# Interleaving the first two output groups of a feed-forward block, and who squares its last step

## The chip, the cores and the metric

The kernel runs on one core of one Trainium2 chip. The metric is the device time of one execution in microseconds; the number compared is the median over several runs. The engines are TensorE (PE in the profile; PEld is its weight load), VectorE (DVE), ScalarE (ACT), GpSimd (POOL) and SyncE (SP), which issues the stores. They run side by side and wait for each other by semaphores.

## What is computed

The input `x` has 8 sequences of 3008 rows of 256 values. The reference takes the Fourier transform along both axes, keeps the real part, and sends each of the 24064 rows through a feed-forward net with squared ReLU:

```python
X = np.fft.fft(np.fft.fft(x, axis=1), axis=2).real    # (8, 3008, 256)
rows = X.reshape(8 * 3008, 256)
h = np.maximum(rows @ w_in, 0.0)                       # (24064, 2048)
out = (h * h) @ w_out                                  # (24064, 256)
```

Matmuls run on 16-bit operands with 32-bit sums; the output is 32-bit.

## The kernel before, in words

*The symmetry.* The real part of the transform of real data needs only half of the rows: row k and its mirror row S - k come from the same two parts, a cosine part C and a sine part Z, one as their sum and one as their difference. The kernel folds each sequence (VectorE, lines 364 to 497), transforms the folded rows with matmuls against sine and cosine tables (`z_steps`, L548) into `zc` and `zs`, and folds the transform along the other axis into `w_in` (`gh`, L499). So FFN1 for the pair of rows is C plus Z for the one and C minus Z for the other.

*Blocks and steps.* The 12040 pairs of rows are cut into 25 blocks `w` (L74, called windows there): 240, 512, 376, 376, 512, 448, then eighteen of 512, and a last one of 360. In a block of n pairs, the hidden layer `h2` is a tile of 128 partitions x 16 chunks x 2n columns: the first n columns of each chunk belong to the one row of the pair (`sg` 0), the next n, in mirrored order, to the other (`sg` 1). FFN1 of a block is eight steps `s` (loop at L965), each making two of the 16 chunks. FFN2 of a block takes groups of 128 columns of `h2` as weights, 16 matmuls of 256 columns per group, one per chunk (L684); it runs one block later. A block of 512 has eight groups; groups 0 to 3 are `sg` 0. `ffn2_steps` (L668) gives a list of jobs of four matmuls, `part(i, hf)` for group i and chunks 4 hf to 4 hf + 3, and `spread` (L713) shares them evenly over the eight steps of the next block: four jobs, so sixteen matmuls, a step. Before the change the jobs stand group after group, so step 0 reads all 16 chunks of group 0, the two chunks of the last block's step 7 among them. Two groups share one PSUM bank `po`, one half each; after the second one's last job ScalarE copies it to `osb` (L699) and SyncE stores it.

*An ordinary step* (L987 on): four matmuls make C + Z in PSUM (`pq`, L831 and L832); ScalarE rectifies it into `sg` 0 (`relu`, L863); FFN2's sixteen matmuls of the step follow (`others`, L881); two turn matmuls (`turn`, L854) take away twice Z in the same PSUM tile; ScalarE rectifies again into `sg` 1. VectorE squares both halves in place in one pass (`power`, L870), which is put off to the next step by `keep` and `settle`.

*A `diff` step* (L967 on), in the steps that the table `diff` (L725) names for a block, saves the turn matmuls. Two matmuls make C (`cosines`, L840); VectorE computes the Nyquist row's share less 2 C into `t2` (`twice`, L844), from products that GpSimd has made before (`nyq_rows`, L792, into one of three buffers `n2`); FFN2's matmuls follow; two matmuls add Z (`sines`, L849); ScalarE rectifies into `sg` 0 (L863), and VectorE adds and rectifies from `t2` and the PSUM tile into `sg` 1 in one custom instruction (L861). VectorE squares `sg` 1 (L870), ScalarE squares `sg` 0 (`power_act`, L874) behind the next step's first rectification (`first`, L876, runs the list `plus`).

*Step 7* is an exception before the change, whichever kind it is, since step 0 of the next block reads its `sg` 0 at once: VectorE squares `sg` 0 right away (`power(s, 0, 1)`, L978 and L994). Where step 7 is a `diff` step, the square of `sg` 1 is put off to step 1 of the next block by the list `defer` (L972, L980, L990).

The PSUM tiles `ph` of the steps come from a pool of two, so a step's first matmuls wait until the tile of the step before the last has been read by both its readers. The steps named by `diff` are 1, 3, 5 and 7 in most blocks, 2, 4 and 6 in blocks 8, 10, 13, 16 and 19 (which carry most of the folding of a new sequence), 1 and 3 in block 9, 4 and 6 in blocks 4 and 5, and 1, 3 and 5 in the last, 24. Every engine's order is that in which the code issues it (`manual_schedule`, L99).

*The start.* While tables are computed and data is loaded, TensorE runs matmuls on zeros whose result nobody reads (`idle`, L293, L296): 28 before the tables, 4 among the small permuting matmuls of the cosine table (`coss`, L259), and 8 behind these, before the first transform (`z0`, L635, matmuls at L569), the products with `w_in` (`gh_step`, L515) and `v_even` (L399), behind which the next sequence is loaded.

*The end.* After the loop, `ffn2_steps(tail=True)` runs the last block's FFN2 (six groups, 96 matmuls), each group with a bank, a copy (L688) and stores of its own.

Of the kernel before, what the change touches and what calls it, by code (L numbers as in the profile page):

```python
# [9 lines left out]
F32 = mybir.dt.float32  # L10
# [6 lines left out]
P = 128  # L17
# [3 lines left out]
def rev_dim(ap, i):  # L21

    dims = [list(d) for d in ap.ap]
    step, cnt = dims[i]
    dims[i] = [-step, cnt]
    return bass.AP(tensor=ap.tensor, offset=ap.offset + step * (cnt - 1), ap=dims)
# [3 lines left out]
def kernel(  # L30
# [14 lines left out]
    nc = tc.nc  # L45
    B, S, D = x.shape
# [8 lines left out]
    NFC = F // P  # L55
# [24 lines left out]
    NW = len(wins)  # L80
# [32 lines left out]
    ps_o = ctx.enter_context(tc.tile_pool(name="ps_o", bufs=2, space=bass.MemoryType.PSUM))  # L113
    ps_z = ctx.enter_context(tc.tile_pool(name="ps_z", bufs=2, space=bass.MemoryType.PSUM))
# [65 lines left out]
    wout16 = const.tile([P, NFC, D], F16, name="wout16")  # L180
# [112 lines left out]
    def idle(n):  # L293

        for i in range(n):
            nc.tensor.matmul(pw[:, 0 : 3 * P], spn[:, 0, 0, :], spn.rearrange("p c r d -> p (c r d)")[:, 0 : 3 * P], start=True, stop=True)  # L296

    idle(28)
    to["args"](0)
    to["args"](1)  # L300
    wd = 2.0 * math.pi / D
# [41 lines left out]
    idle(4)  # L343
    to["coss"](1)
    to["coss"](2)
    idle(8)

    folded = {}

# [278 lines left out]
    def run(*jobs):  # L628
        for j in jobs:
            j()  # L630
# [18 lines left out]
    def store(osb, p0, g0, m, minus, eng=nc.sync):  # L649

        for b, k0, kstep, n, c0 in runs:
            il, ih = max(g0, c0) - c0, min(g0 + m, c0 + n) - 1 - c0
            if minus and k0 in (0, H):
                il = max(il, 1)
            cnt = ih - il + 1
            if cnt <= 0:
                continue
            if minus:
                lo = p0 + (m - 1) - (c0 + ih - g0)
                row = b * S + S - (k0 + kstep * ih)  # L660
            else:
                lo = p0 + c0 + il - g0
                row = b * S + k0 + kstep * il
            eng.dma_start(
                out=bass.AP(tensor=out.tensor, offset=out.offset + row * D, ap=[[kstep * D, cnt], [1, D]]),
                in_=osb[lo : lo + cnt, :])

    def ffn2_steps(w, h2, tail=False):  # L668

        g0, wn = wins[w]  # L670
        groups = [(q, min(P, 2 * wn - q)) for q in range(0, 2 * wn, P)]
        jobs = []
        st = {}

        def part(i, hf):
            q, m = groups[i]
            j = 0 if tail else i % 2
            if tail and hf == 0 and i % 4 > 1:
                st["po"] = ps_z.tile([P, 512], F32, name="po", tag="pz")
            elif j == 0 and hf == 0:  # L680
                st["po"] = ps_o.tile([P, 512], F32, name="po", tag="po")
            po = st["po"]
            for fc in range(hf * 4, hf * 4 + 4):
                nc.tensor.matmul(po[0:m, j * D : (j + 1) * D], h2[:, fc, q : q + m], wout16[:, fc, :], start=(fc == 0), stop=(fc == NFC - 1))  # L684
            if hf == 3 and tail:

                osb = osp.tile([P, 2, D], F32, name="osb", tag="osb")
                nc.scalar.activation(osb[0:m, 0, :], po[0:m, j * D : (j + 1) * D], AF.Copy, bias=0.0, scale=HS * HS)  # L688
                nu = max(0, min(m, wn - q))
                if nu:  # L690
                    store(osb[:, 0, :], 0, g0 + q, nu, False)
                if nu < m:
                    store(osb[:, 0, :], nu, g0 + 2 * wn - q - m, m - nu, True, nc.scalar if i % 2 else nc.sync)
            elif hf == 3 and (j == 1 or i + 1 == len(groups)):
                osb = osp.tile([P, 2, D], F32, name="osb", tag="osb")
                for a, b in ((i - j, i),) if j == 0 or m == P else ((i - 1, i - 1), (i, i)):
                    mm = groups[b][1]
                    lo, hi = (a % 2) * D, (b % 2 + 1) * D
                    nc.scalar.activation(osb[0:mm].rearrange("p s d -> p (s d)")[:, lo:hi], po[0:mm, lo:hi], AF.Copy, bias=0.0, scale=HS * HS)  # L699
                for b in range(i - j, i + 1):  # L700
                    q1, m1 = groups[b]
                    nu = max(0, min(m1, wn - q1))
                    if nu:
                        store(osb[:, b % 2, :], 0, g0 + q1, nu, False)
                    if nu < m1:
                        store(osb[:, b % 2, :], nu, g0 + 2 * wn - q1 - m1, m1 - nu, True)

        for i in range(len(groups)):
            for hf in range(4):
                jobs.append(lambda i=i, hf=hf: part(i, hf))  # L710
        return jobs

    def spread(jobs, i, n):  # L713
# [8 lines left out]
    NST = NFC // 2  # L722
    at_of = {w: [[] for _ in range(NST)] for w in range(NW)}
    post_of = {w: [[] for _ in range(NST)] for w in range(NW)}
    diff = {w: (4, 6) if w < 6 else (1, 3, 5) if w == NW - 1 else (1, 3, 5, 7) for w in range(4, NW)}  # L725
    backs = []

    def put(w, s, i, name, *k, d=at_of):
# [37 lines left out]
    BIG = 3.0e38  # L766
    kept = []
    plus = []
    defer = []

    def settle():
        for k in kept:
            k()
        kept.clear()
        let_go()
# [19 lines left out]
    for w in range(NW):  # L795
        g0, wn = wins[w]
        h2 = h2p.tile([P, NFC, 2 * WN], F16, name="h2", tag="h2")
# [38 lines left out]
        def cosines(s):  # L836
            ph = phs[s] = ps_h.tile([P, 2, 512], F32, name="ph", tag="psh")
            for a in range(2):
                f0 = (2 * s + a) * P
                nc.tensor.matmul(ph[:, a, 0:wn], gh[:, 0, f0 : f0 + P], zcw[:, 0:wn], start=True, stop=True)  # L840

        def twice(s):
            t2 = t2s[s] = tmp.tile([P, 3 * NE], F32, name="t2", tag="tt")[:, 0 : 2 * WN].rearrange("p (a n) -> p a n", a=2)
            nc.vector.scalar_tensor_tensor(out=t2[:, :, 0:wn], in0=phs[s][:, :, 0:wn], scalar=-2.0, in1=n2s[w, s][:, :, 0:wn], op0=ALU.mult, op1=ALU.add)  # L844
# [11 lines left out]
        def relu(s, sg):  # L856
            h = h2[:, 2 * s : 2 * s + 2, sg * wn : (sg + 1) * wn]
            if sg:
                h = rev_dim(h, 2)
            if sg and s in t2s:  # L860
                nc.vector._custom_dve(TENSOR_ADD_SAT, out=h, in0=t2s[s][:, :, 0:wn], in1=phs[s][:, :, 0:wn], s0=BIG, s1=0.0)  # L861
            else:
                nc.scalar.activation(h, phs[s][:, :, 0:wn], AF.Relu, bias=0.0, scale=-1.0)  # L863

        def keep(*k):
            kept.append(lambda p=power: p(*k))

        def power(s, a, b, h2=h2, wn=wn):
            h = h2[:, 2 * s : 2 * s + 2, a * wn : b * wn]
            nc.vector.tensor_tensor(h, h, h, op=ALU.mult)  # L870
# [5 lines left out]
        def first(s):  # L876
            relu(s, 0)
            run(*plus)
            plus.clear()

        def others(s):  # L881
            for j in at[s]:
                j()
            for j in spread(f2, s, NST):
                j()
            for j in post[s]:
                j()
            if s == lo:
                zl[:] = [j for zu, part, h in zj for j in zu(part, h)]
            if s >= lo:  # L890
                for j in spread(zl, s - lo, hi - lo) if s < hi else []:
                    j()
# [72 lines left out]
        for s in range(NST) if w > 1 else ():  # L965
            held["on"] = s + 1 in diff.get(w, ())
            if s in diff.get(w, ()):  # L967
                cosines(s)
                twice(s)
                settle()  # L970
                if s == 1:
                    run(*defer)  # L972
                    defer.clear()
                others(s)
                sines(s)
                first(s)
                if s == NST - 1:
                    power(s, 0, 1)  # L978
                    relu(s, 1)
                    defer.append(lambda p=power, s=s: p(s, 1, 2))  # L980
                else:
                    relu(s, 1)
                    keep(s, 1, 2)
                    plus.append(lambda s=s, p=power_act: p(s))
                nyq(s)
                continue
            pq(s)  # L987
            settle()
            if s == 1:
                run(*defer)  # L990
                defer.clear()
            first(s)
            if s == NST - 1:
                power(s, 0, 1)  # L994
            others(s)
            nyq(s)
            turn(s)
            relu(s, 1)
            keep(s, int(s == NST - 1), 2)
        settle()  # L1000
        old = (w, h2)
    for j in ffn2_steps(*old, tail=True):
        j()

# [29 lines left out]
```

## Time and profile before

| | us |
|---|---|
| three runs: median | 607.11 |
| lowest, highest | 606.73, 608.89 |
| the profiled execution, its own time | 608.64 |
| its span, first to last instruction | 606.9 |
| TensorE's mean granted clock in it | 0.997 |

| group of the page | count | busy us | mean ns |
|---|---|---|---|
| L684 matmul, FFN2 | 3024 | 362.7 | 273 |
| L863 ScalarE, rectification | 312 | 295.2 | 990 |
| L870 VectorE, squares | 216 | 204.9 | 959 |
| L792 GpSimd, Nyquist products | 144 | 150.7 | 1059 |
| L844 VectorE, `twice` | 72 | 86.7 | 1205 |
| L861 VectorE, custom | 67 | 81.6 | 1217 |
| L874 ScalarE, squares | 60 | 63.0 | 1050 |

How to read the lines: a timeline line has the start in us from the span's begin, the length in us, the engine, the line of the kernel (L684), the operation, what is written `<-` what is read, shapes, and the count of merged instructions. Matmuls overlap in the array, so the length of a group is longer than its distance to the next start; distances between starts give the rate. Brackets hold the engine's idle time just before, and what ended it. A line that begins with a range (380.00:400.00) gives that stretch: its length, the busy time of PE, PEld, DVE, ACT and POOL with counts, TensorE's granted clock as a share of full speed, the share of the DMA engines in use, and GB/s.

### The profile page before, as it was taken

What the parts mean: (1) busy time and instruction counts of PE and PEld (TensorE: products, weight loads), DVE (VectorE), ACT (ScalarE), POOL (GpSimd) and SP (SyncE); (2) the same over time, 40 slices, a digit from 0 to 9 for tenths busy, and PEclk for the clock granted to TensorE, in tenths of its full rate; (3) what the DMA queues carried; (4) which work ended last, traced back from release to release, by engine and by line L of the source; (5) the groups of instructions that cost most, each with busy time, mean ns of one, the idle gap of its engine ahead of it and who ended that gap; (6) DMA issues with size and microseconds to landing.
All of it is one profiled execution on the core that took longest, in us unless ns stands there. A gap on an engine that the chain in (4) does not pass through costs nothing.

```text
span 606.9 us, 11251 instructions
## 1 busy us (share of the span) xinstructions
PE 591.3 (97%) x4430; PEld 426.1 (70%) x4430; DVE 486.6 (80%) x591; ACT 445.9 (73%) x601; POOL 232.7 (38%) x266
## 2 busy tenths in 40 slices
PE   6899999999999999999999999999999999999997
PEld 3457777777676777767777767776777776777786
DVE  8787657987889787968998889978899797777760
ACT  6597777967686787777868767778777777686672
POOL 8311223166414605263254550455505723415300
PEclk9999999999999999999999999999999999999999
DMA  8946321137211551272113722147112311221212
GB/s 151 135 88 155 105 81 43 42 104 153 60 45 53 126 136 54 81 166 69 51 46 114 148 62 45 40 123 145 52 36 88 97 44 40 58 54 46 55 55 67
DMA packets 37574, 50.23 MB, mean 83 GB/s; under 512 B 4572, under 2 KB 30721, under 8 KB 37521
## 3 DMA queue, kind: packets, MB, share of 16 engines
q0 software_dynamic: 10352, 24.84, 20.4%
q1 hardware_dynamic: 26899, 24.44, 13.3%
q8 instruction: 34, 0.56, 0.4%
q10 hardware_dynamic: 270, 0.23, 0.1%
q14 instruction: 19, 0.16, 0.1%
HBM read 36.32 MB, written 27.86 MB: 106 GB/s over the span
## 4 chain that ended last, share of the span: by engine, by line
PE 75%; DVE 15%; ACT 5%; issue 3%; DMA 1%; POOL 1%; ACTq 0%; DVEq 0%; POOLq 0%
PE po L684 43%; PE ph L854 6%; PE ph L831 6%; PE ph L832 6%; PE ph L849 5%; PE ph L840 4%; DVE h L870 4%; PE pz L569 4%; DVE h L861 3%; DVE t L844 3%; ACT h L863 2%; DMA xo<-in_x_dram,idx_r 1%; DVE zc L598 1%; DVE zs L598 1%; ACT h L874 1%
## 5 line engine op out<-in xcount | busy, mean ns | idle before, releaser
L684 PE MATMUL po<-wout,h 128*128 128x256 f16 (+1 forms) x3024 | 362.7, 273 | 0.0
L684 PEld LDWEIGHTS <-h 128*128 128x128 f16 (+1 forms) x3024 | 296.3, 98 | 73.0 <-DVE h L870 0.9
L863 ACT ACTIVATE h<-ph 128x1024 f16<-128x1024 f32 (+3 forms) x312 | 295.2, 990 | 60.2 <-PE ph L854 29.3
L870 DVE TENSOR_TENSOR h<-h 128x2048 f16<-128x2048 f16 (+6 forms) x216 | 204.9, 959 | 38.8 <-ACT h L863 35.5
L792 POOL TENSOR_SCALAR n<-zn,g2n 128x512 f32<-128x512 f16 (+2 forms) x144 | 150.7, 1059 | 71.4 <-DMA zn<-rd 35.5
L844 DVE SCALAR_TENSOR_TENSOR t<-ph,n 128x1024 f32<-128x1024 f32 (+2 forms) x72 | 86.7, 1205 | 32.8 <-PE ph L840 28.8
L699 ACT ACTIVATE osb<-po 128x512 f32<-128x512 f32 (+3 forms) x95 | 55.1, 584 | 67.3 <-PE po L684 61.5
L861 DVE CUSTOM_DVE_ANT_0 h<-t,ph 128x1024 f16<-128x1024 f32 x67 | 81.6, 1217 | 18.8 <-ACT h L863 17.7
L831 PE MATMUL ph<-zc,gh 128*128 128x512 f16 (+3 forms) x240 | 88.0, 367 | 0.4 <-ACT h L922 0.3
L832 PE MATMUL ph<-zs,gh 128*128 128x512 f16 (+3 forms) x240 | 88.0, 367 | 0.0
L784 POOL DMA_DIRECT2D zn<-rd x21 | 12.2, 583 | 179.6 <-DMA rd<-zs 179.6
L854 PE MATMUL ph<-zs,gh 128*128 128x512 f16 (+3 forms) x240 | 68.5, 367 | 0.2 <-ACT h L863 0.2
L874 ACT ACTIVATE h<-h 128x1024 f16<-128x1024 f16 (+2 forms) x60 | 63.0, 1050 | 0.0
L840 PE MATMUL ph<-zc,gh 128*128 128x512 f16 (+2 forms) x144 | 42.3, 375 | 1.4 <-DVE h L861 1.3
L849 PE MATMUL ph<-zs,gh 128*128 128x512 f16 (+2 forms) x144 | 42.3, 375 | 1.3 <-DVE t L844 0.4
L832 PEld LDWEIGHTS <-gh 128*128 128x128 f16 x240 | 23.4, 98 | 26.3 <-issue 1.7
L831 PEld LDWEIGHTS <-gh 128*128 128x128 f16 x240 | 23.4, 97 | 25.1
L840 PEld LDWEIGHTS <-gh 128*128 128x128 f16 x144 | 14.0, 98 | 19.5 <-issue 4.1
L854 PEld LDWEIGHTS <-gh 128*128 128x128 f16 x240 | 22.3, 98 | 4.2 <-issue 0.3
L574 ACT ACTIVATE es<-pz 128x376 f32<-128x376 f32 (+1 forms) x32 | 14.8, 485 | 9.7 <-PE pz L569 9.5
L453 POOL DMA_DIRECT2D scr<-ev x8 | 4.7, 590 | 42.4 <-DVE ev L449 36.7
L132 POOL DMA_INDIRECT xo<-in_x_dram,idx_r x15 | 18.0, 1202 | 4.5 <-issue 4.3
(141 smaller groups left out, 358.6 us busy)
## 6 DMA issues: line engine op xcount, KB each, us to landing
out_dram<-osb SPq DMA_DIRECT2D x77, 128.0 KB
xo<-in_x_dram POOLq DMA_DIRECT2D x7, 768.0 KB
scr<-ev POOLq DMA_DIRECT2D x8, 390.0 KB
zn<-rd POOLq DMA_DIRECT2D x19, 128.0 KB
rb<-scr POOLq DMA_DIRECT2D x16, 130.0 KB
out_dram<-osb SPq DMA_DIRECT2D x12, 94.0 KB
w<-in_moe_w_in_dram POOLq DMA_DIRECT2D x2, 512.0 KB
wout<-in_moe_w_out_dram POOLq DMA_DIRECT2D x1, 1024.0 KB
```

Of the source, the lines that this page charges most:

```text
L684: nc.tensor.matmul(po[0:m, j * D : (j + 1) * D], h2[:, fc, q : q + m], wout16[:, fc, :], start=(fc == 0), stop=(fc == NFC - 1))
L792: nc.gpsimd.tensor_scalar(out=n2[:, a, 0:wn1], in0=zns[wt][:, 0:wn1], scalar1=g2n[:, fc : fc + 1], scalar2=1.0, op0=ALU.mult, op1=ALU.mult)
L831: nc.tensor.matmul(ph[:, a, 0:wn], gh[:, 0, f0 : f0 + P], zcw[:, 0:wn], start=True, stop=False)
L832: nc.tensor.matmul(ph[:, a, 0:wn], gh[:, 1, f0 : f0 + P], zsw[:, 0:wn], start=False, stop=True)
L840: nc.tensor.matmul(ph[:, a, 0:wn], gh[:, 0, f0 : f0 + P], zcw[:, 0:wn], start=True, stop=True)
L844: nc.vector.scalar_tensor_tensor(out=t2[:, :, 0:wn], in0=phs[s][:, :, 0:wn], scalar=-2.0, in1=n2s[w, s][:, :, 0:wn], op0=ALU.mult, op1=ALU ...
L849: nc.tensor.matmul(phs[s][:, a, 0:wn], gh[:, 1, f0 : f0 + P], zsw[:, 0:wn], start=False, stop=True, skip_group_check=True)
L854: nc.tensor.matmul(phs[s][:, a, 0:wn], gh[:, 2, f0 : f0 + P], zsw[:, 0:wn], start=False, stop=True, skip_group_check=True)
L861: nc.vector._custom_dve(TENSOR_ADD_SAT, out=h, in0=t2s[s][:, :, 0:wn], in1=phs[s][:, :, 0:wn], s0=BIG, s1=0.0)
L863: nc.scalar.activation(h, phs[s][:, :, 0:wn], AF.Relu, bias=0.0, scale=-1.0)
L870: nc.vector.tensor_tensor(h, h, h, op=ALU.mult)
L874: nc.scalar.activation(h, h, AF.Square, bias=0.0, scale=1.0)
```

## The change

It has four parts. (1) In `ffn2_steps` the jobs of groups 0 and 1 are interleaved: chunks 0 to 11 of group 0, chunks 0 to 11 of group 1, then chunks 12 to 15 of both. At four jobs a step, step 0 gets chunks 0 to 11 of group 0 and 0 to 3 of group 1, and step 1 the rest. Both sums of the bank are then open at once; group 1's first matmul no longer starts the bank afresh (`start`), since group 0's has. The tail uses the same order with a bank for each group. (2) Step 7 of a `diff` block becomes an ordinary `diff` step: ScalarE squares `sg` 0 by way of `plus`, which step 0 of the next block runs behind its first rectification (after the last block it is run ahead of the tail), and VectorE squares `sg` 1 by `keep`, which `settle` runs at the end of the block. `defer` is gone. (3) The last block's `diff` becomes 1, 3, 5, 7. (4) The warm-up matmuls are 34 instead of 28 at the first place and 5 instead of 8 at the last.

```diff
-    idle(28)
+    idle(34)
...
-    idle(8)
+    idle(5)
...
             if tail and hf == 0 and i % 4 > 1:
-                st["po"] = ps_z.tile([P, 512], F32, name="po", tag="pz")
+                st["po", i] = ps_z.tile([P, 512], F32, name="po", tag="pz")
             elif j == 0 and hf == 0:
-                st["po"] = ps_o.tile([P, 512], F32, name="po", tag="po")
-            po = st["po"]
+                st["po", i] = ps_o.tile([P, 512], F32, name="po", tag="po")
+            po = st["po", i - j]
+            both = i == 1 and not tail
             for fc in range(hf * 4, hf * 4 + 4):
-                nc.tensor.matmul(..., start=(fc == 0), stop=(fc == NFC - 1))
+                nc.tensor.matmul(..., start=(fc == 0 and not both), stop=(fc == NFC - 1), skip_group_check=i < 2)
...
-        for i in range(len(groups)):
-            for hf in range(4):
-                jobs.append(lambda i=i, hf=hf: part(i, hf))
+        order = [(0, 0), (0, 1), (0, 2), (1, 0), (1, 1), (1, 2), (0, 3), (1, 3)]
+        for i, hf in order + [(i, hf) for i in range(2, len(groups)) for hf in range(4)]:
+            jobs.append(lambda i=i, hf=hf: part(i, hf))
...
-    diff = {w: (4, 6) if w < 6 else (1, 3, 5) if w == NW - 1 else (1, 3, 5, 7) for w in range(4, NW)}
+    diff = {w: (4, 6) if w < 6 else (1, 3, 5, 7) for w in range(4, NW)}
...
                 settle()
-                if s == 1:
-                    run(*defer)
-                    defer.clear()
                 others(s)
                 sines(s)
                 first(s)
-                if s == NST - 1:
-                    power(s, 0, 1)
-                    relu(s, 1)
-                    defer.append(lambda p=power, s=s: p(s, 1, 2))
-                else:
-                    relu(s, 1)
-                    keep(s, 1, 2)
-                    plus.append(lambda s=s, p=power_act: p(s))
+                relu(s, 1)
+                keep(s, 1, 2)
+                plus.append(lambda s=s, p=power_act: p(s))
                 nyq(s)
...
         settle()
         old = (w, h2)
+    run(*plus)
     for j in ffn2_steps(*old, tail=True):
```

An ordinary step 7 (`pq`, L987 on) keeps its `power(s, 0, 1)` on VectorE.

More of the change, by code (lines that the diff above doesn't have):

```diff
@@ L678, in part @@
             if tail and hf == 0 and i % 4 > 1:
-                st["po"] = ps_z.tile([P, 512], F32, name="po", tag="pz")
+                st["po", i] = ps_z.tile([P, 512], F32, name="po", tag="pz")
             elif j == 0 and hf == 0:
-                st["po"] = ps_o.tile([P, 512], F32, name="po", tag="po")
-            po = st["po"]
+                st["po", i] = ps_o.tile([P, 512], F32, name="po", tag="po")
+            po = st["po", i - j]
+            both = i == 1 and not tail
             for fc in range(hf * 4, hf * 4 + 4):
-                nc.tensor.matmul(po[0:m, j * D : (j + 1) * D], h2[:, fc, q : q + m], wout16[:, fc, :], start=(fc == 0), stop=(fc == NFC - 1))
+                nc.tensor.matmul(po[0:m, j * D : (j + 1) * D], h2[:, fc, q : q + m], wout16[:, fc, :], start=(fc == 0 and not both), stop=(fc == NFC - 1), skip_group_check=i < 2)
             if hf == 3 and tail:
@@ L768 @@
     plus = []
-    defer = []
     def settle():
@@ L988 @@
             settle()
-            if s == 1:
-                run(*defer)
-                defer.clear()
             first(s)
```

## The prediction

> **What bounds the kernel now.** I read the page first, for the shares of the engines, and then one window of steady work.
>
> ```profile
> span 606.9 us, 11251 instructions
> PE 591.3 (97%) x4430; PEld 426.1 (70%) x4430; DVE 486.6 (80%) x591; ACT 445.9 (73%) x601; POOL 232.7 (38%) x266
> 380.00:400.00 20.00, 19.98 (x163) 14.85 (x162) 19.47 (x20) 14.75 (x22) 6.60 (x7) 1.00 0.19 60
> ```
>
> TensorE is the bound: it is busy for 19.98 of 20 us there, while VectorE (19.47) runs just below it and ScalarE (14.75) has room. So a gain can come only from matmuls that go, or from places where TensorE stands still. I looked for those in TensorE's timeline, by comparing each start with the one before plus the steady rate. The rates come from the rows at the boundary between two blocks at 355 us, where step 7 of one block is of the `diff` kind (sixteen FFN2 matmuls, L684, take 361.36 - 359.62 = 1.74 us, and a pair of 512-wide ones 361.79 - 361.36 = 0.43):
>
> ```profile
> 356.45 2.00 PE L684 MATMUL po<-wout,h 128*128 128x256 f16 x16
> 358.29 0.59 PE L854 MATMUL ph<-zs,gh 128*128 128x512 f16 x2
> 359.19 0.59 PE L840 MATMUL ph<-zc,gh 128*128 128x512 f16 x2 [0.30 <-DVE h L861]
> 359.62 1.91 PE L684 MATMUL po<-wout,h 128*128 128x256 f16 x16
> 361.36 0.59 PE L849 MATMUL ph<-zs,gh 128*128 128x512 f16 x2
> 361.79 0.38 PE L831 MATMUL ph<-zc,gh 128*128 128x512 f16 x1
> ```
>
> Step 0's sixteen took 358.29 - 356.45 = 1.84, 0.10 over the rate. Step 1's cosine pair (L840) could have begun at 358.29 + 0.43 = 358.72, and began at 359.19: 0.47 late, and its row names VectorE's L861. VectorE and ScalarE at the same place:
>
> ```profile
> 356.84 1.16 DVE L870 TENSOR_TENSOR h<-h 128x1024 f16<-128x1024 f16 x1 [0.61 <-ACT h L863]
> 357.93 1.21 DVE L861 CUSTOM_DVE_ANT_0 h<-t,ph 128x1024 f16<-128x1024 f32 x1
> 359.89 1.23 DVE L844 SCALAR_TENSOR_TENSOR t<-ph,n 128x1024 f32<-128x1024 f32 x1 [0.75 <-PE ph L840]
> 355.79 1.94 ACT L863 ACTIVATE h<-ph 128x1024 f16<-128x1024 f32 x2
> 358.92 1.02 ACT L863 ACTIVATE h<-ph 128x1024 f16<-128x1024 f32 x1 [1.20 <-PE ph L854]
> 363.86 1.07 ACT L874 ACTIVATE h<-h 128x1024 f16<-128x1024 f16 x1
> ```
>
> This is the mechanism. Step 7's rectified half comes from ScalarE (first of the two at 355.79, done at about 356.8). VectorE, idle till then, squares it (L870, 1.16 us), because step 0's FFN2 reads it at once; only then does it run L861, the last reader of step 7's buffer in PSUM, which step 1 needs. TensorE waits for both. ScalarE meanwhile is idle for 1.20 us.
>
> **The change part by part.**
>
> *The squares at a boundary.* There are twelve boundaries whose step 7 is of the `diff` kind (blocks 6, 7, 11, 12, 14, 15, 17, 18 and 20 to 23). At each, VectorE loses one L870 in front of L861. L861 still cannot begin before ScalarE's first half is read, but follows it directly: at 356.84 instead of 357.93, 1.09 us earlier. So it ends near 358.0, before TensorE is there at 358.7, and the 0.47 goes whole. The gaps before step 1, each worked out as above, are 0.14, 0.11, 0.21, 0.18, 0.47, 0.18, 0.47, 0.00, 0.46, 0.13, 0.14 and 0.53; the first and the last of the twelve:
>
> ```profile
> 163.38 0.59 PE L854 MATMUL ph<-zs,gh 128*128 128x512 f16 x2
> 163.95 0.59 PE L840 MATMUL ph<-zc,gh 128*128 128x512 f16 x2
> 573.43 0.47 PE L854 MATMUL ph<-zs,gh 128*128 128x360 f16 x2
> 574.26 0.47 PE L840 MATMUL ph<-zc,gh 128*128 128x360 f16 x2 [0.36 <-DVE h L861]
> 453.14 0.69 DVE L870 TENSOR_TENSOR h<-h 128x1024 f16<-128x1024 f16 x1 [0.61 <-ACT h L863]
> 502.03 2.00 PE L684 MATMUL po<-wout,h 128*128 128x256 f16 x16
> ```
>
> They sum to **3.0 us**. None is larger than the least that L861 gains: the square at 453.14, with nothing beside it on GpSimd, takes 0.6 to 0.7. The 0.10 in step 0's FFN2 stands at four boundaries (a row of 2.00 instead of 1.91; 356.45 is the second, 502.03 the last): **0.4 us**; it goes because chunks 12 to 15 are read in step 1, eight matmuls in (after 359.6).
>
> What comes in their place: ScalarE makes that square (L874, 1.07) after step 0's first rectification, from about 357.7 to 358.8. Queued behind it is step 0's second rectification, which waits for L854 until 358.92 anyway; so its cover is the 1.20 us idle, and if it were gone, up to 1.07 us of delay would meet step 2, which wants that PSUM buffer only at 361.79, nearly two us after it is freed. I cost it at nothing, and no block has more ScalarE work in step 0 ahead of that point. The second half's square (VectorE) moves from step 1 to directly behind L861. Queued behind it is step 1's L844, for which TensorE's L849 waits. It would run from about 358.0 to 358.6, or 359.1 at the 1.16 of the row above; L844 is due 0.7 after its cosines start (359.19 to 359.89), now 359.3. It fits by 0.2 to 0.7 us. The matmuls of groups 0 and 1 are as many as before, into the same bank; the first output copy still follows group 1's last matmul at the end of step 1, so output stores (SP's queue) do not move. Nothing in the trace prices two open sums in one bank; the nearest rows are FFN2's own, at the same rate whichever half they write, so between nothing and a few ns each, and I take nothing.
>
> *Block 8.* VectorE is the late one there, and this changes what is queued:
>
> ```profile
> 189.28 1.90 DVE L870 TENSOR_TENSOR h<-h 128x2048 f16<-128x2048 f16 x2 [0.32 <-ACT h L863]
> 191.11 1.37 DVE L424 TENSOR_TENSOR fo<-xo 128x1536 f16<-128x1536 f16 x1
> 192.40 1.21 DVE L844 SCALAR_TENSOR_TENSOR t<-ph,n 128x1024 f32<-128x1024 f32 x1
> 191.60 1.91 PE L684 MATMUL po<-wout,h 128*128 128x256 f16 x16
> 193.66 0.59 PE L849 MATMUL ph<-zs,gh 128*128 128x512 f16 x2
> ```
>
> The second of the two squares at 189.28 is the one deferred from block 7. Moved ahead, it lets L844 begin about 0.6 earlier, and the wait of 193.66 - 191.60 - 1.75 = 0.31 us before L849 goes: **0.3 us**.
>
> *The last block.* Its step 7 becomes `diff`: two turn matmuls (L854) leave TensorE.
>
> ```profile
> 591.67 0.47 PE L854 MATMUL ph<-zs,gh 128*128 128x360 f16 x2
> 591.98 10.64 PE L684 MATMUL po<-wout,h 128*128 128x256 f16 x96
> 588.34 0.82 ACT L874 ACTIVATE h<-h 128x720 f16<-128x720 f16 x1
> 587.84 0.90 DVE L861 CUSTOM_DVE_ANT_1 h<-t,ph 128x720 f16<-128x720 f32 x1 [1.24 <-ACT h L863]
> ```
>
> That is 591.98 - 591.67 = **0.3 us**. In exchange one L844 and one L861 (0.90) run on VectorE instead of a ScalarE pass, and ScalarE squares the first half after the loop (0.82). The tail now begins with 24 matmuls (24 x 0.109 = 2.6 us) that need neither; rectification and square are two ScalarE passes behind the sines, each about as long as that 0.82, so 1.8 with their starts. GpSimd makes one more pair of products, off the path at 38%. Cost nothing; if the cover failed, at most the difference between one pass and the 2.6 us, below 1 us, once.
>
> *The warm-up matmuls.*
>
> ```profile
> 1.22 7.11 PE L296 MATMUL pw<-spn 128*128 128x384 f16 x28 [1.22 <-DVE spn L188]
> 14.13 2.56 PE L296 MATMUL pw<-spn 128*128 128x384 f16 x8
> 16.53 0.64 PE L569 MATMUL pz<-cos,od 128*128 128x376 f16 x3
> 17.01 0.59 PE L515 MATMUL pg<-w,c_all 128*128 128x512 f16 x2
> 15.07 0.22 ACT L396 ACTIVATE od<-cs 128x6 f16<-128x6 f16 x1
> 12.00:14.00 2.00, 1.31 (x6) 0.48 (x5) 1.93 (x4) 2.00 (x3) 1.73 (x10) 0.74 1.01 145
> 14.00:16.00 2.00, 2.00 (x8) 0.88 (x6) 1.96 (x3) 1.10 (x3) 1.86 (x3) 0.50 1.12 206
> 16.00:18.00 2.00, 2.00 (x13) 1.05 (x12) 0.57 (x1) 0.48 (x1) 0.99 (x4) 0.91 1.27 193
> 35.67 0.22 DVE L419 COPY fe<-xo 128x24 f16<-128x24 f16 x1 [1.59 <-DMA xo<-in_x_dram,idx_r]
> 11.13 0.48 PE L259 MATMUL pc<-sin,perm 128*128 128x376 f16 x2 [2.80 <-ACT sin L249]
> ```
>
> The six that are added run where TensorE stands idle for 2.80 us; even at 0.32 us each (2.56 over 8) they end before 11.13 and cost nothing. The eight lie on the path at half clock (0.50), for their successor's operands are there at 15.29 (L396's end) and it starts at 16.53. With five, it starts at 14.13 + 5 x 0.32 = 15.73. The clock row 0.91 puts full speed at about 16.4, so two of its three matmuls then run at 0.31 and it ends at 16.5 instead of 17.01: **0.5 us**. What follows hangs on it, down to the load that ends at 35.67, for which VectorE waited 1.59, so the half us goes through.
>
> [...]
>
> *Sum*: 3.0 + 0.4 + 0.3 + 0.3 + 0.5 = 4.5 us. The profiled execution took 608.64 us with a span of 606.9, and would take 604.1; the median shown, 607.11, becomes **602.6 us**.
>
> **The rivals.**
>
> *The clock stays up (0.2).* If 34 instead of 28 keep it at full until 16.4, the five end before 15.0, and L569 starts when L396 is done, at 15.3, and ends at 15.8: 1.2 gained instead of 0.5, so 601.9. [...]
>
> *The wait moves (0.15).* The square behind L861 delays L844, and the boundary's gap stands before L849 instead of before L840. For it: only 0.2 us of room where GpSimd works beside it. The 3.0 is lost and the rest kept: 605.6.
>
> *Slower, by L861 not moving (0.05).* If L861 were held until 357.93 by something other than the removed square, it would end as before and now have 0.6 to 1.16 us more between it and L844. From the point where L861 gains less than about 0.3, every added bit shows on TensorE: 3.4 kept as stalls and 12 x 0.7 added, less 1.1 from the rest: about 614. Against it: the 357.93 row has no idle of its own, it stood directly behind the square.
>
> *No effect (0.05)*: step 1 is late for another reason and only the first and last terms count, 606.3.
>
> **How the numbers follow.** Forecast 0.55, at 602.6. The low end lets the clock stay up and a little more of VectorE's lateness go: 600.9. The high end takes in the moved wait: 605.6. Half a per cent, about what a measurement of this kernel can tell from no change, is 3.0 us, so below 604.1 counts as faster: 0.55 + 0.2, and a little of the moved wait where it is partial, 0.76; within, 0.19; slower, 0.05.
>
> **What would show it.** Right: at the boundary L861 directly behind ScalarE's first half, L874 in ScalarE's gap, L840 within 0.05 of L854's end, no gap before L849 of step 1; 24 matmuls of the tail without a pause; L569 at 15.7. Wrong: L849 waiting for L844 in step 1, L684 in step 1 waiting for L874, or L569 starting no earlier than 16.5.

## The result, and the profile after

| | before, us | after, us |
|---|---|---|
| median (6 runs each) | 607.26 | 602.64 |
| lowest, highest | 606.73, 608.89 | 602.50, 603.37 |
| span of the profiled execution | 606.9 | 600.7 |

The ratio is 0.992, with a 95% interval of 0.9905 to 0.9936: 4.6 us faster. Run again beside the kernel before in a later set (`e5_after_again`, below), it is 602.55 against 607.69, 5.1 us. The profile is of the execution that took 602.58 us.

In the page, TensorE keeps its share, VectorE has eleven instructions less and ScalarE twelve more:

```profile
span 600.7 us, 11246 instructions
PE 587.6 (98%) x4431; PEld 426.4 (71%) x4431; DVE 479.9 (80%) x580; ACT 456.7 (76%) x613; POOL 227.9 (38%) x268
```

The boundary of blocks 14 and 15 again, in TensorE's timeline (the new kernel's FFN2 line is L685):

```profile
353.91 1.91 PE L685 MATMUL po<-wout,h 128*128 128x256 f16 x16
355.66 0.59 PE L854 MATMUL ph<-zs,gh 128*128 128x512 f16 x2
356.09 0.59 PE L840 MATMUL ph<-zc,gh 128*128 128x512 f16 x2
356.52 1.91 PE L685 MATMUL po<-wout,h 128*128 128x256 f16 x16
358.27 0.59 PE L849 MATMUL ph<-zs,gh 128*128 128x512 f16 x2
```

Step 1's cosine pair starts 0.43 after L854, which is the rate itself: no gap, and step 0's sixteen take 1.75 again. VectorE and ScalarE there:

```profile
354.36 1.22 DVE L861 CUSTOM_DVE_ANT_0 h<-t,ph 128x1024 f16<-128x1024 f32 x1 [0.80 <-ACT h L863]
355.62 0.69 DVE L870 TENSOR_TENSOR h<-h 128x1024 f16<-128x1024 f16 x1
356.79 1.23 DVE L844 SCALAR_TENSOR_TENSOR t<-ph,n 128x1024 f32<-128x1024 f32 x1 [0.49 <-PE ph L840]
353.31 1.94 ACT L863 ACTIVATE h<-ph 128x1024 f16<-128x1024 f32 x2
355.12 1.07 ACT L874 ACTIVATE h<-h 128x1024 f16<-128x1024 f16 x1
356.29 1.02 ACT L863 ACTIVATE h<-ph 128x1024 f16<-128x1024 f32 x1
```

L861 waits for ScalarE alone. The square behind it is done at about 356.3, and L844 then waits for TensorE (0.49 idle), so the square cost nothing. ScalarE's square fills its gap: the next rectification follows at 356.29, and the step that needs its buffer starts at about 358.7.

To see where the 6.2 us between the two spans come from, I took the start of the first matmul of each of the 184 steps of blocks 2 to 24 in both timelines, and the change of their difference from step to step:

| stretch | gained, us |
|---|---|
| the start, up to block 2 (52.01 against 50.84) | 1.17 |
| wait before step 1, twelve `diff` boundaries (step 0's 0.1 included) | 3.40 |
| block 8, before steps 3 and 5 | 0.49 |
| waits at block 15 step 0 and block 17 steps 5 and 6 | 0.64 |
| after the last step's start | 0.46 |

They add up to 6.2. The profiled execution of the kernel before took 608.64, 1.4 above the median of its runs, so 6.2 is too much for the change; the experiments separate the two. The waits at block 17 (0.46 of the 0.64) come and go, with the change and without it: the profiles of runs 1, 7, 8, 9, 10 and 11 have them, those of runs 2, 3, 4, 5 and 6 have not.

### The profile page after: what moved, and what is told of

Its sections match the earlier page's. It is cut to its first block, busy times and chain, and to the rows that moved or that the text cites. A ratio compares the mean times of both kernels' runs of the same rounds, so it can differ in the third digit from the quotient of the medians.

```text
span 600.7 us, 11246 instructions
## 1 busy us (share of the span) xinstructions
PE 587.6 (98%) x4431; PEld 426.4 (71%) x4431; DVE 479.9 (80%) x580; ACT 456.7 (76%) x613; POOL 227.9 (38%) x268
## 4 chain that ended last, share of the span: by engine, by line
PE 79%; DVE 12%; ACT 4%; issue 2%; DMA 1%; POOL 1%; DVEq 0%; ACTq 0%; POOLq 0%
PE po L685 46%; PE ph L854 7%; PE ph L831 7%; PE ph L832 7%; PE ph L849 5%; PE ph L840 4%; PE pz L569 4%; DVE h L870 3%; DVE t L844 2%; DVE h L861 2%; ACT h L863 2%; DMA xo<-in_x_dram,idx_r 1%; ACT h L874 1%; DVE zc L598 1%; DVE zs L598 1%
## 5 line engine op out<-in xcount | busy, mean ns | idle before, releaser
L685 PE MATMUL po<-wout,h 128*128 128x256 f16 (+1 forms) x3024 | 362.3, 273 | 0.0
L685 PEld LDWEIGHTS <-h 128*128 128x128 f16 (+1 forms) x3024 | 296.8, 98 | 72.0
L870 DVE TENSOR_TENSOR h<-h 128x1024 f16<-128x1024 f16 (+6 forms) x203 | 196.0, 971 | 28.2 <-ACT h L863 25.2
L792 POOL TENSOR_SCALAR n<-zn,g2n 128x512 f32<-128x512 f16 (+2 forms) x146 | 146.7, 1017 | 70.7 <-DMA zn<-rd 48.4
L844 DVE SCALAR_TENSOR_TENSOR t<-ph,n 128x1024 f32<-128x1024 f32 (+2 forms) x73 | 87.7, 1202 | 31.8 <-PE ph L840 30.7
L861 DVE CUSTOM_DVE_ANT_0 h<-t,ph 128x1024 f16<-128x1024 f32 x67 | 81.7, 1219 | 31.3 <-ACT h L863 29.7
L874 ACT ACTIVATE h<-h 128x1024 f16<-128x1024 f16 (+2 forms) x73 | 76.6, 1049 | 0.0
L854 PE MATMUL ph<-zs,gh 128*128 128x512 f16 (+3 forms) x238 | 68.1, 367 | 0.2 <-ACT h L863 0.2
L849 PE MATMUL ph<-zs,gh 128*128 128x512 f16 (+2 forms) x146 | 42.8, 374 | 1.0 <-DVE t L844 0.4
L840 PEld LDWEIGHTS <-gh 128*128 128x128 f16 x146 | 14.2, 98 | 16.8 <-issue 0.3
L854 PEld LDWEIGHTS <-gh 128*128 128x128 f16 x238 | 22.1, 98 | 4.1 <-issue 0.3
L463 POOL DMA_INDIRECT rb<-scr,idx_r x16 | 17.8, 1111 | 4.9 <-issue 4.9
```

The lines of the kernel that those rows point to most:

```text
L792: nc.gpsimd.tensor_scalar(out=n2[:, a, 0:wn1], in0=zns[wt][:, 0:wn1], scalar1=g2n[:, fc : fc + 1], scalar2=1.0, op0=ALU.mult, op1=ALU.mult)
L849: nc.tensor.matmul(phs[s][:, a, 0:wn], gh[:, 1, f0 : f0 + P], zsw[:, 0:wn], start=False, stop=True, skip_group_check=True)
L854: nc.tensor.matmul(phs[s][:, a, 0:wn], gh[:, 2, f0 : f0 + P], zsw[:, 0:wn], start=False, stop=True, skip_group_check=True)
L874: nc.scalar.activation(h, h, AF.Square, bias=0.0, scale=1.0)
```

## The experiments

Twelve runs, in three sets. The kernel before ran beside each set, and its median there is named, since it differs by set: 607.90 in the first, 607.69 in the second, 607.63 in the third.

**1. The squares without the warm-ups.**

```diff
-    idle(34)
+    idle(28)
...
-    idle(5)
+    idle(8)
```

> The changed kernel with the warm-up matmuls as they were (28 and 8). By the forecast the warm-up part is worth 0.5 us, so 603.1. A rival, from the two profiles: their 1.2 us apart at 52 us is mostly where the half-clock stretch happened to fall, and the median loses little: 602.6 to 602.9, with executions up to 1.5 us above the lowest as the kernel before has them. If the warm-ups were worth the whole 1.2 us: 603.8.

Measured: 603.36 (602.60 to 604.39), ratio 0.9926 (0.9902 to 0.995), 4.5 below before. Across sets it is 0.7 to 0.8 above the changed kernel. Its steps gain 3.4 at the boundaries, and in the tail 0.5, as in the changed kernel. So the squares, block 8 and the last block carry most of the change. The value lies between the forecast's 603.1 and the largest one, and the six runs spread over 1.8 us. Its profile reaches block 2 at 51.05, against 52.01 before: 0.96 of the 1.17 that the table gives to the start came here with the old warm-ups; by its clock rows the half-clock stretch lay from about 11.3 to 14.7, earlier than before.

**2. The warm-ups alone**, in the kernel before: `idle(34)` and `idle(5)`.

> The kernel before with 34 and 5 warm-up matmuls and nothing else. Forecast: 0.5 us below the kernel before, 606.8. Rival (half-clock stretch falls by chance): lowest executions unchanged near 606.7, the slow ones near 608.8 gone or fewer, median 606.5 to 607.1. If the warm-ups were worth 1.2: 606.0.

Measured: 606.85 (605.66 to 607.81), ratio 0.9981 (0.9967 to 0.9995): 1.05 below before, with 0.3 to 2.0 as the interval. In its profile the clock never fell. The two rows that read 0.74 and 0.50 before:

```profile
12.00:14.00 2.00, 1.19 (x7) 0.52 (x6) 1.93 (x4) 2.00 (x3) 1.73 (x10) 1.00 1.09 138
14.00:16.00 2.00, 1.56 (x11) 0.73 (x9) 1.97 (x3) 1.03 (x4) 1.86 (x3) 1.00 1.04 194
```

That is the rival of the clock that stays up, in this one execution: its first transform starts at 15.29, limited by its operand. In the changed kernel's own profile the clock fell earlier, and was back earlier:

```profile
10.00:12.00 2.00, 0.86 (x3) 0.49 (x4) 2.00 (x4) 1.90 (x3) 2.00 (x3) 0.72 1.08 205
12.00:14.00 2.00, 2.00 (x8) 0.95 (x7) 1.93 (x4) 1.64 (x3) 1.73 (x10) 0.50 1.06 142
14.00:16.00 2.00, 1.73 (x10) 0.81 (x9) 1.96 (x3) 1.46 (x3) 1.86 (x3) 0.93 1.07 196
15.52 0.65 PE L569 MATMUL pz<-cos,od 128*128 128x376 f16 x3 [0.27 <-ACT od L396]
```

There the transform starts at 15.52, all three matmuls at full speed. Where the half-clock stretch lies differs from execution to execution: by the clock rows it is about 13.0 to 16.4 in the profile of the kernel before, 11.3 to 14.7 in that of run 1, 10.9 to 14.3 in the changed kernel's, and in this one there is none.

How far the warm-ups reach differs as well. Their first group in the changed kernel's profile (34), in this one (34) and in that of run 7 (42):

```profile
1.22 7.07 PE L296 MATMUL pw<-spn 128*128 128x384 f16 x34 [1.22 <-DVE spn L188]
1.22 8.60 PE L296 MATMUL pw<-spn 128*128 128x384 f16 x34 [1.22 <-DVE spn L188]
1.22 8.61 PE L296 MATMUL pw<-spn 128*128 128x384 f16 x42 [1.22 <-DVE spn L188]
```

The first 9 to 19 of them start 0.32 us apart and the others 0.16, so 34 end at 8.3 us in one execution and at 9.8 in another, as late as 42 do in a third. Of the fourteen profiles of this case, the ten in which this group ends by 9.6 us have a half-clock stretch behind it, and the four in which it ends at 9.8 or later (runs 2, 7, 8 and 10) have none.

The profile of this run shows a wait that the change was not thought to touch. Block 19 has an ordinary step 7, and at its boundary with block 20 this kernel of the old order stood still for 1.31 us. The square that TensorE needed there, step 7's, was short, but it was queued on VectorE behind step 6's, which took 3.73 us instead of 0.69. TensorE, VectorE and GpSimd:

```profile
478.01 0.39 PE L684 MATMUL po<-wout,h 128*128 128x256 f16 x2 [1.31 <-DVE h L870]
473.62 3.73 DVE L870 TENSOR_TENSOR h<-h 128x1024 f16<-128x1024 f16 x1
472.78 4.03 POOL L792 TENSOR_SCALAR n<-zn,g2n 128x512 f32<-128x512 f16 x6
```

GpSimd's six products run back to back, 0.67 us each, and VectorE's square ends only half a us after the last.

**3. ScalarE's square, but group after group.**

```diff
-        order = [(0, 0), (0, 1), (0, 2), (1, 0), (1, 1), (1, 2), (0, 3), (1, 3)]
+        order = [(i, hf) for i in range(2) for hf in range(4)]
```

> The changed kernel with FFN2's jobs group after group again, so step 0 reads step 7's squares at once while ScalarE still makes them. Theory (the later read is what gives ScalarE the time): TensorE needs the square 14 matmuls into step 0, about 0.8 us before ScalarE has it, at twelve boundaries, so 0.6 to 0.9 each: 610 to 613. Rival (taking the square from VectorE is enough by itself): 602.6 to 603.

Measured: 613.17 (612.57 to 613.28), ratio 1.0082 (1.0051 to 1.0113), 5.3 slower than before and, across sets, 10.6 above the changed kernel; just above the range expected. At the boundary of blocks 14 and 15, TensorE and ScalarE:

```profile
357.55 1.69 PE L685 MATMUL po<-wout,h 128*128 128x256 f16 x14
359.88 0.39 PE L685 MATMUL po<-wout,h 128*128 128x256 f16 x2 [0.64 <-ACT h L874]
358.75 1.07 ACT L874 ACTIVATE h<-h 128x1024 f16<-128x1024 f16 x1
```

Fourteen matmuls in, TensorE waits for the square, as worked out. Beside the changed kernel's profile, the twelve boundaries lose 9.5 us, 0.8 each, and the tail, which reads step 7's squares early too, 0.5 more, which the forecast had left out. Moving the work to the idle engine loses without the later read.

**4. The interleaved order alone**, in the kernel before (VectorE still squares ahead of L861, `defer` stays):

```diff
+        order = [(0, 0), (0, 1), (0, 2), (1, 0), (1, 1), (1, 2), (0, 3), (1, 3)]
```

> The kernel before with only the two groups interleaved: VectorE still squares ahead of its custom instruction. Theory (the gap before step 1 is set by the custom instruction behind the square): only the 0.1 us inside step 0 goes, at four or five boundaries, so 0.4 to 0.5 below before, 606.8. Rival (the wait was for the squares to be read): most of the 3.4 us goes, 603.9.

Measured: 607.25 (605.89 to 610.07), ratio 0.9986 (0.9965 to 1.0006): unclear by itself, but not the rival's 603.9. Its profile shows the wait where it was (L841 is `cosines`, L862 the custom instruction, L864 the rectification, L871 the square in this kernel):

```profile
356.51 1.91 PE L685 MATMUL po<-wout,h 128*128 128x256 f16 x16
359.25 0.59 PE L841 MATMUL ph<-zc,gh 128*128 128x512 f16 x2 [0.40 <-DVE h L862]
356.90 1.16 DVE L871 TENSOR_TENSOR h<-h 128x1024 f16<-128x1024 f16 x1 [0.61 <-ACT h L864]
357.99 1.21 DVE L862 CUSTOM_DVE_ANT_0 h<-t,ph 128x1024 f16<-128x1024 f32 x1
```

The 0.1 inside step 0 is gone and has gone into the gap: the custom instruction ends at the same time, so TensorE only waits later, and the 0.4 expected is not in this profile: its twelve boundaries gain nothing in sum. Neither half of the change works alone.

**5. The changed kernel again**, as the base of the second set.

> The changed kernel once more, as the base of this set: 602.5 to 603.4. In its profile the waits before step 1 should again be nothing, wherever the half-clock stretch of the start falls.

Measured: 602.55 (602.17 to 603.05), ratio 0.9903 (0.988 to 0.9926); 3.4 gained at the boundaries in its profile. By the share of its clock rows (0.85 for 12 to 14, 0.79 for 16 to 18) the clock fell at about 13.4 and was back at about 16.8, so this is nearly the start that the forecast drew: L569 at 15.74, at half speed.

**6. VectorE squares both halves behind L861.**

```diff
-                keep(s, 1, 2)
-                plus.append(lambda s=s, p=power_act: p(s))
+                keep(s, int(s < NST - 1), 2)
+                if s < NST - 1:
+                    plus.append(lambda s=s, p=power_act: p(s))
```

> The changed kernel, but VectorE squares both halves of step 7 in one pass behind its custom instruction, and ScalarE makes no square there. Theory (the gain is that nothing stands ahead of the custom instruction, not who squares): the custom instruction is as early as in the changed kernel, the one pass of 1.2 us behind it delays step 1's L844 by 0.0 to 0.4 at the tighter boundaries, so 602.6 to 605. Rival (ScalarE's taking the work is what counts): back to near the warm-up-only time, 606.9.

Measured: 603.90 (603.26 to 604.80), ratio 0.9929 (0.9906 to 0.9953), 1.35 above the changed kernel and 3.8 below before. VectorE and TensorE at the boundary of blocks 14 and 15, and then in the tail:

```profile
354.56 1.22 DVE L861 CUSTOM_DVE_ANT_0 h<-t,ph 128x1024 f16<-128x1024 f32 x1 [0.54 <-ACT h L863]
355.82 1.23 DVE L870 TENSOR_TENSOR h<-h 128x2048 f16<-128x2048 f16 x1
356.99 1.22 DVE L844 SCALAR_TENSOR_TENSOR t<-ph,n 128x1024 f32<-128x1024 f32 x1
358.47 0.59 PE L849 MATMUL ph<-zs,gh 128*128 128x512 f16 x2
589.23 7.80 PE L685 MATMUL po<-wout,h 128*128 128x256 f16 x70 [0.18 <-DVE h L870]
```

The boundaries gain 3.4 here too, so what counts there is that no square stands ahead of the custom instruction, not who makes it. In the tail TensorE waits for the square, and from the last step's start to the end this profile takes 0.5 longer than the changed kernel's; block 8 loses 0.14 before step 5. The rest of the 1.35 is not in this profile (its execution, 603.26, was the lowest of six).

**7 and 8. The idle stretch of the start filled**: `idle(42)` with 5, and `idle(42)` with 8.

> The changed kernel with 42 instead of 34 warm-up matmuls, which reach to about 10.6 us and nearly fill the idle stretch. Theory (half clock comes from the idle stretch between the warm-ups and the table's matmuls): clock 1.00 from 10 us on, the first transform at 15.3, the execution 0.2 to 0.8 below the changed kernel beside it, near 602.2, and less spread. Rival (34 are enough, the rest is chance): no difference.

> 42 and 8 warm-up matmuls. Theory: at full clock eight take 1.3 us from 13.9, so they end before the operands of the first transform are there at 15.3, and the time is that of 42 and 5. If the clock still falls to half, the eight are 1 us late again and the median lies 0.5 above 42 and 5.

Measured: 602.56 (602.16 to 603.05) and 602.41 (602.24 to 602.99), against 602.55 for the changed kernel. The clock did stay up, here with 42 and 5, and the first transform started at 15.29 in both:

```profile
12.00:14.00 2.00, 1.19 (x7) 0.52 (x6) 1.93 (x4) 2.00 (x3) 1.73 (x10) 1.00 1.05 162
14.00:16.00 2.00, 1.56 (x11) 0.73 (x9) 1.97 (x3) 1.03 (x4) 1.86 (x3) 1.00 1.11 207
16.00:18.00 2.00, 1.80 (x12) 0.87 (x11) 1.70 (x4) 0.98 (x3) 1.00 (x4) 1.00 1.30 198
```

So filling the stretch does hold the clock, and eight matmuls then are as good as five: the mean granted clock is 0.999 or 1.000 in all twelve executions, against two of the six with 34 (run 5). The 42 end at 9.8 and 10.3 us, not at the 10.6 expected. But the time is the same, and so is the spread; in run 5 too, the two executions at full clock (602.17, 602.84) are no faster than the other four. In the profiles, `e7_fill_42` is 1.0 us ahead of `e5_after_again` at block 2 and 0.5 ahead at the end, with 0.47 lost in block 17. The half us that should remain is no more than the runs differ by, and six runs of each do not show it. No version ran that is clearly faster than the changed kernel.

**9. The second half's square put off to step 1 again**, by `defer` as before the change:

```diff
-                keep(s, 1, 2)
+                if s == NST - 1:
+                    defer.append(lambda p=power, s=s: p(s, 1, 2))
+                else:
+                    keep(s, 1, 2)
```

> The changed kernel, but the square of step 7's second half waits till step 1 of the next block, as before the change, instead of standing between the custom instruction and step 1's L844. Forecast (it fits into the room there and is free): the same as the changed kernel but for block 8, where the 0.5 us comes back, so 602.6 to 603.2. Rival (the wait moves to L844): clearly below the changed kernel, 601.5 or less.

Measured: 603.43 (602.92 to 604.11), 0.9 above the changed kernel of the second set, where up to 0.65 was expected. Against the changed kernel's profile its boundaries neither gain nor lose (under 0.05), block 8 loses 0.33 and 0.18 before steps 3 and 5, and block 17 the 0.46 that comes and goes. The rival of the moved wait is refuted, and block 8's gain comes from this move.

**10. The last block's steps 1, 3 and 5 only.**

```diff
-    diff = {w: (4, 6) if w < 6 else (1, 3, 5, 7) for w in range(4, NW)}
+    diff = {w: (4, 6) if w < 6 else (1, 3, 5) if w == NW - 1 else (1, 3, 5, 7) for w in range(4, NW)}
```

> The changed kernel with the last block's steps 1, 3, 5 as before, so its step 7 has its two turn matmuls again. Forecast: 0.3 us above the changed kernel; by the two profiles' ends, which lie 0.5 further apart than their last steps: 0.5 above, 603.0 to 603.2. Rival (hidden anyway): no difference.

Measured: 603.06 (602.56 to 603.36), 0.5 above the changed kernel of the second set, with ranges that overlap; the profile has 0.5 too behind the last step's start.

**11. The kernel of 2 once more**, a single run (its label does not fit: GpSimd's work is not doubled here).

> The kernel before with 34 and 5 warm-up matmuls once more, one look: whether the wait of 1.3 us for VectorE's square that its first profile had in block 20 is there again. Theory (it is a collision of VectorE's squares with GpSimd's products, which falls differently in each execution): not at the same place, or of another length; the six boundaries behind an ordinary step 7 and the twelve behind a diff step 7 together wait 3 to 6 us. Rival (a fixed wait of this kernel): 1.3 us in block 20 again.

Measured: one run, 606.80; block 20's wait is not there. The longest 1024-wide L870 in its profile took 1.16 us, not 3.73. The waits up to step 1 at the twelve boundaries sum to 3.0 here, 3.4 in the first profile and 2.9 in run 2, whose 1.47 of block 20 comes on top; the six behind an ordinary step 7 wait no longer here than in the changed kernel. It began as the changed kernel's profile did (50.73 and 50.84 at block 2) and its span, 605.0, is 4.3 longer. That is near what the change is worth without the start, but 0.46 of it is the wait at block 17 that comes and goes.

**12. GpSimd's products twice in the changed kernel**: the line L792 written two times.

> The changed kernel with each of GpSimd's Nyquist products made twice. Theory (GpSimd's products stretch VectorE's squares, and at a boundary the changed kernel has room for that): VectorE's squares get longer on the mean by 0.1 us or more, yet step 0 and step 1 wait less than 1 us in all twelve; the time grows by VectorE's lateness inside the blocks, 1 to 6 us. Rival (no collision between the two engines): squares as long as before, time the same.

Measured: 610.78 (609.45 to 612.49), 8.2 above the changed kernel. Both theories miss. VectorE's squares hardly lengthen (1024-wide ones 756 ns on the mean instead of 735, 2048-wide ones 1311 instead of 1255), yet the time grows by more than expected, since `twice` (L845 here) waits for the products themselves. From the view of that line:

```profile
  POOL n L793: 25.0, 15
  PE ph L850: 4.4, 8
```

VectorE idles 25.0 us for the second product in 15 places, and TensorE waits behind it. What did hold is that steps 0 and 1 wait nowhere even so: 3.4 gained there as ever. The means do not settle whether VectorE's squares and GpSimd's products collide, but the single squares do: in the fourteen profiles, of the 755 1024-wide squares that ran with no product beside them none took over 0.77 us, and of the 443 with a product beside them 178 took over 0.80 (in this run's profile none of 34 and 19 of 49).

## Why the prediction was right, point by point

The forecast of 602.6 met 602.64. The mechanism and the largest term were right; that the time fits to 0.04 us is luck. Three smaller terms came out larger in the runs, that of the warm-ups with a wide interval, and the median of the kernel before, from which the sum is taken, lay between 607.11 and 607.90 in its sets, so that the same change measures 4.6 us in one set and 5.1 in another. By its steps:

*The squares at a boundary*: 3.0 + 0.4 forecast, 3.4 in the changed kernel's profile, and the sum over the steps 1 of all blocks is 3.4 in the profiles of all nine kernels that keep L861 free of squares and FFN2's later read. The mechanism is shown from both sides: with the square back ahead of L861 the gap is back (run 4), with it behind L861 on either engine it is gone (runs 5 and 6). That the later read is what makes ScalarE's square free is run 3, at 10.6 us. The square in front of L844 is free (run 9): L844 has 0.49 us of room behind it in the profile after, within the 0.2 to 0.7 worked out. Two open sums in one bank cost nothing that shows: sixteen FFN2 matmuls take 1.75 us either way.

*Block 8*: 0.3 forecast, 0.49 measured. The term was mis-sized, because I stopped at the wait before step 3; VectorE, once ahead, also removes the one of 0.18 before step 5. Step 4 before, then steps 2 and 4 after:

```profile
197.56 1.91 PE L684 MATMUL po<-wout,h 128*128 128x256 f16 x16
199.54 0.59 PE L849 MATMUL ph<-zs,gh 128*128 128x512 f16 x2
190.19 1.91 PE L685 MATMUL po<-wout,h 128*128 128x256 f16 x16
191.94 0.59 PE L849 MATMUL ph<-zs,gh 128*128 128x512 f16 x2
195.84 1.91 PE L685 MATMUL po<-wout,h 128*128 128x256 f16 x16
197.64 0.59 PE L849 MATMUL ph<-zs,gh 128*128 128x512 f16 x2
```

The distance between the two starts falls from 1.98 to 1.80 in step 4, and in step 2 to the rate, 1.75.

*The last block*: 0.3 forecast, 0.5 measured by runs and profiles. TensorE's part is the 0.30 of the two turn matmuls, and the cover held: the tail's 96 matmuls run without a pause (`585.99 10.64 PE L685`, as long as before). The other 0.2 lies between the last copy's start and the end of the span (4.2 us before, 4.1 after) and is not explained.

*The warm-up matmuls*: 0.5 forecast, 1.05 measured in the kernel before, with a wide interval, and 0.7 to 0.8, across sets, in the changed kernel (run 1). The step's picture of one place for the half-clock stretch failed: the profile that I worked from was one execution, and others have it elsewhere, or not at all. Of the 50 executions of the kernel before beside the three sets, eleven had a mean granted clock of 0.993 to 0.995, and they took 608.2 to 611.4 us, all above the median of their set. In the changed kernel's twelve none lies below 0.996. The clock is not all of it: others of the 50 took up to 610.3 at 0.996 or more.

*The sum against one execution.* I took 4.5 from an execution 1.4 above the median, and the difference of the profiles was 6.2, while that of the medians was 4.6. The sum suited the medians; by the profiles alone it would have been short by 1.7. Most of that is chance of the two executions: up to 0.96 at the start (run 1) and 0.46 at block 17. The changed kernel also spreads less: its two sets of six runs cover 0.9 us each, the six of the kernel before beside the first 2.2. Why is not shown.

*The rivals*: the clock that stays up occurs (run 2), without an effect that medians resolve (run 7). The wait that moves (no gap before L849 in the profile after, and run 9), L861 that does not move (the profile after) and the one of no effect (3.4 gained at the boundaries) are refuted.

## What to carry to other kernels

When the bound engine waits at a seam for the last reader of a buffer, look at what stands ahead of that reader on its own engine; often a consumer can be shifted by one step, so that the work in front can go behind, or to an engine with a gap. Shift the read first: moving the work alone made it slower here (613.17). And compare medians with sums from one profiled execution only after looking at what differs between executions of the same kernel.

## What the runs showed of the hardware

A VectorE multiply of two 16-bit operands in SBUF, 0.69 us with no GpSimd product beside it (the row at 453.14 in the profile before), took 3.73 us in run 2 while GpSimd ran six element-wise products back to back. It began at 473.62, during the second product, and ended at 477.35, half a us behind the sixth. The counts under run 12 say the same of single squares: none of 755 took over 0.77 us with no product beside it, 178 of 443 took over 0.80 with one. What in the hardware makes them collide is not shown. The profile of the kernel before has the same place, 2 us later:

```profile
475.85 1.77 DVE L870 TENSOR_TENSOR h<-h 128x1024 f16<-128x1024 f16 x2
475.05 5.48 POOL L792 TENSOR_SCALAR n<-zn,g2n 128x512 f32<-128x512 f16 x6
```

Here the six products took 5.48 us instead of 4.03, and two squares together 1.77, so here GpSimd's products lengthened more than VectorE's squares; which engine loses differs between these two executions.

TensorE's half-clock stretch at the start, 3.4 us long in the profiles of the kernel before, the changed kernel and runs 1 and 5, began at 13.0 us in the first, at 10.9 and 13.4 in the changed kernel's two (the first profile and run 5), and did not come in run 2, with the same or nearly the same instructions; in the four profiles whose first warm-up matmuls ended at 9.8 us or later (runs 2, 7, 8 and 10) there was none. What sets its place is not shown.
